# Moving a dispatch by four columns, splitting a weight conversion in three steps, and one stream for the expert weights

## The chip, the cores and the metric

The kernel runs on one core of one Trainium2 chip. The metric is the device time of one execution in microseconds (us); lower is better. The engines are PE (TensorE), DVE (VectorE), ACT (ScalarE), POOL (GpSimd) and SP (SyncE, which here only issues transfers).

## The reference

Three stages follow one another, all in float32. `q`, `k`, `v` are (8, 8, 576, 64); `T` is 4608 tokens, the model width is 512.

```
scores = scale * q_chunk @ k_chunk.T         # chunks of 64 tokens, each on its own
attn   = softmax(scores); x = attn @ v_chunk # -> x: (4608, 512)
h = x @ w_in                                 # (512, 2048)
g = h * sigmoid(1.702 * h)
y = g @ w_out                                # (2048, 512)
logits = y @ phi                             # 32 slots: 8 experts x 4
d = softmax(logits, axis=tokens)             # dispatch
slot_in  = d.T @ y                           # (32, 512)
slot_out = relu(slot_in[e] @ w1[e]) @ w2[e]  # each expert, 1024 wide
out = softmax(logits, axis=slots) @ slot_out # combine
```

## The kernel before, in words

**Blocks and columns.** The 4608 tokens are twelve blocks of 384 tokens. A block runs sixteen *columns* `f`, one for each 128 of the 2048 hidden units. `gemm(b, f)` (line 270) is 12 matmuls into one of three `h` banks (high part of the weight by high and low part of x, low part of the weight by high part of x), then a Tanh on ACT (L278) and one DVE instruction (L279) make the gated value. In the tables and in this text 2.4 is block 2, column 4.

**Order.** For the head and blocks 0 to 10 the order of instructions on each engine is the program's order. The tables `HEAD`, `SIDE0`, `SIDE1`, `SIDE2` (for the head and blocks 0 to 2) and `PLAN` (from block 2 on) say which extra step follows which column; `start` (L769) and `side` (L702) read them. In the last block and the tail only SP's order is given by hand. Each engine works strictly in order, so a step that waits holds all that stands behind it on its engine.

**Attention.** Three chunk pairs (`cp`) make a block. Scores (`attn_s`, L203) go to a pair tile `sx` of two banks, DVE takes the maximum and subtracts it (L211, L212), ACT takes Exp (L220), DVE sums, adds epsilon and inverts (L222 to L225), POOL or DVE multiplies (L226), PE transposes (L237), ACT copies, PE multiplies by v (`attn_x`, L251), ACT and DVE write the high and low part of x (L264, L265). In the head, `two_scores` (L763, step `R`) puts the scores of pairs 0 and 1 in one pair tile, so each bank holds both pairs.

**Conversion of w_in.** The weights come as 64-bit words. `w_in_a` (L141): ACT L118, then DVE L119 (shift) and L122 (shift and or). `w_in_b` (L144): ACT L147 copies the high part, POOL L148 subtracts it to make the low part. In block 0, column f is followed by `w_in_b(f+3)` and then `w_in_a(f+4)` (L798 to L802). The steps `i` and `j` in `HEAD` are the same two. `start_sel` (step `s`, L740) builds a small selection matrix on DVE; it is first used in 1.3.

**Dispatch.** g of a finished block is transposed on DVE (L289), stored to DRAM (L296, SP), read back in another layout (`load_g`, L304, four transfers of 768 KB on SP), and multiplied by the slot weights in `dispatch` (L468): 12 times two PE instructions, whose first ones read the transfer that was issued last. Block 0's `load_g` stands behind 2.0 and its dispatch, step `D`, behind 2.4. Block 1's stand behind 2.5 (`g0`) and 2.12 (`d0`); for later blocks it is the same two columns of the block that follows.

**Expert weights.** `load` (L517) fills a tile with the next units of `units` (the order in which the tail reads them); each run of neighbouring units in `w1` or `w2` is a transfer of its own, nearly all issued by POOL (L539, L545). w1 and w2 lie in DRAM as [128, expert, ...], each partition's row 128 KiB long. `TABLE` says where tiles are loaded; in the tail `used` (L551) refills a tile when its last unit is read. `combine` (L676) runs once for each half of the output: PE L688, copies on DVE and ACT, and six transfers of 768 KB, on POOL for the first half and on SP for the second.

Of the kernel before, what the change touches and what calls it, by code (L numbers as in the profile page):

```python
# [8 lines left out]
F32 = mybir.dt.float32  # L9
# [27 lines left out]
HEAD = "z q0 q1 q2 Li0 v0 v1 v2 Li1 R e0 i0 P2,- e1 i1 b0 j0 e2r P-,0 b1 j1 b2 P-,1 P-,2 Li2 q3 Li3 v3 Li4 q4 i2 j2 i3"  # L37
SIDE0 = {
    0: "P3,- Li5 v4 Li6", 1: "e3 q5", 2: "Li7 v5", 3: "P4,- b3 Li8", 4: "e4 phi Li9", 5: "Li10 q6", 6: "P5,3 Li11 v6",
    7: "e5 b4 Li12", 8: "Li13 q7", 9: "P6,4 Li14 v7", 10: "e6 b5 Li15", 11: "s Lo0r", 12: "P7,5 Lo1r", 13: "e7 b6 Lo2r", 14: "Lo3r",  # L40
# [7 lines left out]
SIDE2 = {0: "S2 g", 1: "S3", 3: "S4", 4: "D"}  # L48
# [4 lines left out]
def attention_moe_softmoe_kernel(  # L53
# [8 lines left out]
    w1: bass.AP,  # L62
    w2: bass.AP,
# [5 lines left out]
    E, F = w1.shape[1], w1.shape[2] * 128  # L69
# [7 lines left out]
    KE = F // 128  # L77
# [37 lines left out]
    def to_f32(a, st):  # L115
        f = st.bitcast(F32).rearrange("p (n w) -> p n w", w=2)
        u = st.bitcast(U32).rearrange("p (n w) -> p n w", w=2)
        nc.scalar.activation(out=a, in_=f[:, :, 1], func=ACTF.Prelu, scale=2.0 ** -112, alpha=-(2.0 ** 32))  # L118
# [768 lines left out]
```

## Time and profile before

| what | us |
|---|---|
| median of 3 runs (lowest to highest) | 682.08 (681.12 to 682.31) |
| the profiled execution | 681.62 |
| its span, first to last instruction | 679.8 |
| PE busy | 619.9 |
| DVE busy | 453.2 |

Times of instructions are counted from the start of the span. A bracket behind a row of a timeline is the idle time of that engine just before, and what ended it.

### The profile page before, as it was taken

How to read it: one execution, taken by the hardware profiler on the slowest of the kernel's cores; microseconds unless marked ns; L12 is line 12 of the kernel's file. 1: busy time of each engine (PE TensorE's matmuls, PEld its weight loads, DVE VectorE, ACT ScalarE, POOL GpSimd, SP SyncE). 2: the span in 40 equal slices, each digit the busy share in tenths (PEclk: the TensorE clock that was granted, in tenths of full speed). 3: DMA queues.
4: the chain of work that ended last, by engine and by line, in shares of the span. 5: the costliest groups of instructions: out<-in, count | busy, mean ns of one | idle time of the engine just before them, and what ended most of it. 6: DMA issues, size and time to landing. Idle time of an engine off the chain costs nothing.

```text
span 679.8 us, 15616 instructions
## 1 busy us (share of the span) xinstructions
PE 619.9 (91%) x6414; PEld 522.1 (77%) x6414; DVE 453.2 (67%) x972; ACT 225.6 (33%) x469; POOL 115.2 (17%) x160
## 2 busy tenths in 40 slices
PE   3797899994999999999999999999999999978891
PEld 3685766792989899898998998989989898736550
DVE  5688789791867778778677786776876736331132
ACT  3446444330324234233333332323423322111141
POOL 2253300000100000000000010000010222454640
PEclk9999999996999999999999999999999999999996
DMA  9934867669656749478486585774938879889998
GB/s 348 352 94 140 279 189 247 182 152 350 234 170 225 247 147 347 120 230 285 136 290 210 160 322 157 237 234 151 346 97 230 292 233 396 295 276 369 369 402 341
DMA packets 67798, 167.94 MB, mean 247 GB/s; under 512 B 13200, under 2 KB 36880, under 8 KB 67728
## 3 DMA queue, kind: packets, MB, share of 16 engines
q1 hardware_dynamic: 57376, 129.72, 57.8%
q0 software_dynamic: 10352, 37.23, 15.0%
q8 instruction: 50, 0.82, 0.5%
q14 instruction: 20, 0.16, 0.1%
HBM read 122.29 MB, written 44.63 MB: 246 GB/s over the span
## 4 chain that ended last, share of the span: by engine, by line
PE 77%; DVE 10%; DMA 5%; ACT 3%; issue 2%; POOL 0%; SPq 0%; DVEq 0%; ACTq 0%; POOLq 0%
PE h L274 18%; PE h L276 17%; PE h L275 17%; PE dtg L474 5%; PE lp L340 5%; PE sx L203 3%; DVE cv L122 2%; PE sx L251 2%; PE h1p L635 2%; PE pt L237 2%; DVE cv L119 2%; DMA g<-g_dram 1%; DVE gt L279 1%; DMA out_dram<-o 1%; PE fp L655 1%
## 5 line engine op out<-in xcount | busy, mean ns | idle before, releaser
L274 PE MATMUL h<-xh,w 128*128 128x384 f32 x768 | 266.0, 346 | 3.1 <-ACT w L147 2.4
L276 PE MATMUL h<-xh,w 128*128 128x384 f32 x768 | 258.8, 337 | 7.4 <-POOL w L148 7.4
L275 PE MATMUL h<-xl,w 128*128 128x384 f32 x768 | 258.0, 336 | 0.0
L278 ACT ACTIVATE gt<-h 128x384 f32<-128x384 f32 x192 | 94.1, 490 | 234.5 <-PE h L276 234.3
L274 PEld LDWEIGHTS h<-xh,w 128*128 128x128 f32 x768 | 144.7, 188 | 22.6 <-issue 17.5
L279 DVE SCALAR_TENSOR_TENSOR gt<-gt,h 128x384 f32<-128x384 f32 x192 | 104.9, 547 | 82.8 <-ACT gt L278 82.4
L276 PEld LDWEIGHTS h<-xh,w 128*128 128x128 f32 x768 | 144.7, 188 | 10.2 <-POOL w L148 9.3
L275 PEld LDWEIGHTS h<-xl,w 128*128 128x128 f32 x768 | 144.9, 189 | 0.4 <-DVE xl L265 0.4
L226 POOL TENSOR_TENSOR e<-e,rs 128x512 f32<-128x512 f32 x35 | 36.6, 1047 | 443.5 <-DVE rs L225 440.9
L289 DVE STREAM_TRANSPOSE g<-gt 128x384 f32<-128x384 f32 x176 | 100.1, 574 | 5.4
L264 ACT ACTIVATE xh<-sx 128x512 fp32r<-128x512 f32 x36 | 21.5, 599 | 95.8 <-DVE e L212 82.2
L474 PE MATMUL dtg<-g,dt 128*32 128x512 f32 x288 | 35.1, 622 | 10.5 <-DMA g<-g_dram 9.1
L265 DVE TENSOR_TENSOR xl<-sx,xh 128x512 fp32r<-128x512 f32 x36 | 24.8, 690 | 26.6 <-ACT xh L264 24.5
L340 PE MATMUL lp<-gt,wp 128*32 128x384 f32 x384 | 36.8, 492 | 0.1
L474 PEld LDWEIGHTS dtg<-g,dt 128*32 128x32 f32 x288 | 9.5, 114 | 30.8 <-issue 29.2
L539 POOL DMA_DIRECT2D w<-in_moe_w_dram x44 | 23.6, 542 | 53.4 <-PE h L276 23.6
L545 POOL DMA_DIRECT2D w<-in_moe_w_dram x53 | 28.4, 538 | 17.6 <-DMA w<-in_moe_w_dram 10.3
L211 DVE TENSOR_REDUCE mx<-sx 128x8 f32<-128x512 f32 x36 | 23.7, 659 | 7.0 <-PE sx L203 7.0
L122 DVE SCALAR_TENSOR_TENSOR cv<-stg,cv 128x512 uint32<-128x512 uint32 x32 | 27.2, 851 | 1.1
L148 POOL TENSOR_TENSOR w<-cv,w 128x512 fp32r<-128x512 f32 x16 | 22.9, 1443 | 23.7 <-ACT w L147 23.7
L237 PE MATMUL pt<-ident,e 128*128 128x128 f32 x144 | 23.1, 286 | 3.7 <-POOL e L226 2.1
L212 DVE TENSOR_TENSOR e<-sx,mx 128x512 f32<-128x512 f32 x36 | 24.9, 691 | 1.8
(118 smaller groups left out, 560.5 us busy)
## 6 DMA issues: line engine op xcount, KB each, us to landing
g_dram<-g SPq DMA_DIRECT2D x176, 192.0 KB, 3.7
g<-g_dram SPq DMA_DIRECT2D x44, 768.0 KB, 8.3
w<-in_moe_w_dram POOLq DMA_DIRECT2D x70, 256.0 KB, 5.5
qk<-in_qk_dram SPq DMA_DIRECT2D x30, 512.0 KB, 5.6
w<-in_moe_w_dram POOLq DMA_DIRECT2D x27, 512.0 KB, 7.3
stg<-in_moe_w_in_dram SPq DMA_DIRECT2D x16, 512.0 KB, 8.2
stg<-in_moe_w_out_t_dram SPq DMA_DIRECT2D x16, 512.0 KB, 5.5
wo<-in_moe_w_out_dram SPq DMA_DIRECT2D x16, 512.0 KB, 3.7
```

What stands on the lines that cost most here:

```text
L122: nc.vector.scalar_tensor_tensor(out=a.bitcast(U32), in0=u[:, :, 0], scalar=29, in1=a.bitcast(U32), op0=ALU.logical_shift_right, op1=ALU.b ...
L226: (nc.gpsimd if pool else nc.vector).tensor_tensor(out=e, in0=e, in1=rs.to_broadcast([128, 2 * KD, 64]), op=ALU.mult)
L237: nc.tensor.transpose(p[:, hp, :], e[:, 2 * hp:2 * hp + 2, :].rearrange("p h k -> p (h k)"), ident)
L274: nc.tensor.matmul(out=h, lhsT=a, rhs=xh[b][:, k, :], start=(k == 0), stop=False)
L275: nc.tensor.matmul(out=h, lhsT=a, rhs=xl[b][:, k, :], start=False, stop=False)
L276: nc.tensor.matmul(out=h, lhsT=l, rhs=xh[b][:, k, :], start=False, stop=(k == KD - 1))
L278: nc.scalar.activation(out=t, in_=h, func=ACTF.Tanh, scale=0.851)
L279: nc.vector.scalar_tensor_tensor(out=t, in0=t, scalar=1.0, in1=h, op0=ALU.add, op1=ALU.mult)
L289: nc.vector.transpose(out=g1[b, q][:, :, :, 32 * j:32 * (j + 1)], in_=t.rearrange("p (a b c) -> p b a c", b=4, c=32))
L340: nc.tensor.matmul(out=lp[b][32 * j:32 * (j + 1), :], lhsT=wp[:, f, :], rhs=gt[b, f], start=(g == 0), stop=(g == NG - 1),)
L474: nc.tensor.matmul(out=p[32 * j:32 * (j + 1)], lhsT=dt[:, i, :], rhs=g[j][i], start=(i == 0), stop=(i == NCP - 1))
L545: eng.dma_start(out=v, in_=w2[:, key[1], key[2], c:c + m])
```

## The change

- `D` moves from behind 2.4 to behind 2.8; in block 2 alone `g0` moves from column 5 to 9 and `d0` from 12 to 15.
- The conversion of w_in is three steps: `w_in_a` (ACT L118), `w_in_b` (the two DVE instructions), `w_in_c` (ACT copy, POOL subtraction). Behind column f of block 0 stand a(f+5), b(f+4), c(f+3), in that order; the transfers of the weights stand up to one column earlier.
- In the head `R` is replaced by `A0 A1r A2` (scores) and `C0r C1 C2r` (products with v). Those with `r` use two `h` banks, and their evictions go in two halves, one for each bank; the others use the pair tile. The multiplications of pairs 0 and 1 (`e0r`, `e1r`) go from POOL to DVE. The conversion of the second weight tile stands behind `C2r`.
- `start_sel` moves from 0.11 to 1.1, with one broadcast copy in place of four.
- w1 and w2 become one array w12 of [128, 65536] in the order of use; `load` issues one transfer for a tile. Each partition's row is now 256 KiB long.

The core of the diff (left out: the arguments of the kernel, `attn_x`, which indexes its two banks the same way as `attn_s`, and the lines of `start` that call `first`):

```diff
@@ -34,18 +34,18 @@
...
-HEAD = "z q0 q1 q2 Li0 v0 v1 v2 Li1 R e0 i0 P2,- e1 i1 b0 j0 e2r P-,0 b1 j1 b2 P-,1 P-,2 Li2 q3 Li3 v3 Li4 q4 i2 j2 i3"
+HEAD = "z q0 q1 q2 Li0 v0 v1 v2 Li1 A0 A1r i0 e0r A2 e1r I0 b0 e2r j0 C0r i1 b1 C1 b2 C2r I1 j1 Li2 q3 Li3 v3 Li4 q4 i2 i3 I2 j2 i4 I3"
 SIDE0 = {
-    0: "P3,- Li5 v4 Li6", 1: "e3 q5", 2: "Li7 v5", 3: "P4,- b3 Li8", 4: "e4 phi Li9", 5: "Li10 q6", 6: "P5,3 Li11 v6",
-    7: "e5 b4 Li12", 8: "Li13 q7", 9: "P6,4 Li14 v7", 10: "e6 b5 Li15", 11: "s Lo0r", 12: "P7,5 Lo1r", 13: "e7 b6 Lo2r", 14: "Lo3r",
+    0: "P3,- Li5 v4 Li6 Li7", 1: "e3 q5", 2: "Li8 v5", 3: "P4,- b3 Li9", 4: "e4 phi Li10", 5: "Li11 q6", 6: "P5,3 Li12 v6",
+    7: "e5 b4 Li13", 8: "Li14 q7", 9: "P6,4 Li15 v7", 10: "e6 b5", 11: "Lo0r", 12: "P7,5 Lo1r", 13: "e7 b6 Lo2r", 14: "Lo3r",
     15: "Lo4r",
...
 SIDE1 = {
-    0: "o0 o1 Lo5r Lo6r", 1: "o2 o3 Lo7r Lo8r", 2: "b7 c0 o4 o5 Lo9r Lo10r", 3: "d0 o6 o7 Lo11r Lo12r", 4: "P8,6 k0 l0 c1 o8 Lo13r",
+    0: "o0 o1 Lo5r Lo6r", 1: "s o2 o3 Lo7r Lo8r", 2: "b7 c0 o4 o5 Lo9r Lo10r", 3: "d0 o6 o7 Lo11r Lo12r", 4: "P8,6 k0 l0 c1 o8 Lo13r",
     5: "e8 d1 o9 o10 Lo14r Lo15r", 6: "o11 o12", 7: "c2 o13 o14 t0 t1", 8: "P9,7 k1 l1 d2 o15", 9: "e9 c3 t2 t3 t4", 10: "b8 d3 t5 t6 t7",
...
 }
-SIDE2 = {0: "S2 g", 1: "S3", 3: "S4", 4: "D"}
+SIDE2 = {0: "S2 g", 1: "S3", 3: "S4", 8: "D"}
 EPS = 1e-9
@@ -113,9 +111,15 @@
...
+        to_f32_a(a, st)
+        to_f32_b(a, st)
...
+    def to_f32_a(a, st):
...
+        nc.scalar.activation(out=a, in_=f[:, :, 1], func=ACTF.Prelu, scale=2.0 ** -112, alpha=-(2.0 ** 32))
...
+    def to_f32_b(a, st):
...
-        nc.scalar.activation(out=a, in_=f[:, :, 1], func=ACTF.Prelu, scale=2.0 ** -112, alpha=-(2.0 ** 32))
@@ -139,9 +143,13 @@
...
     def w_in_a(f):
-        iv[f] = conv("i", f)
+        iv[f] = pro[0].tile([128, DM], F32, tag="cv", name="cv", bufs=NCV)
+        to_f32_a(iv[f], stg["i", f])
...
     def w_in_b(f):
+        to_f32_b(iv[f], stg.pop(("i", f)))
+
+    def w_in_c(f):
         v = iv.pop(f).rearrange("p (k c) -> p k c", k=KD)
@@ -192,27 +200,34 @@
...
+    def each(p):
+        return [(slice(h, h + 1), p[h].rearrange("p (o x) -> p o x", o=1)) for h in range(2)] if isinstance(p, list) else [(slice(0, 2), p)]
...
-        p = p.rearrange("p h (a k) -> p h a k", k=64)
+        y = [p[h] if isinstance(p, list) else p[:, h, :] for h in range(2)]
+        y = [v.rearrange("p (a k) -> p a k", k=64) for v in y]
...
-                        out=p[w, h, hp, :], lhsT=t[r, 0, hp, w], rhs=t[r, 1, hp, w], start=True, stop=True
+                        out=y[h][w, hp, :], lhsT=t[r, 0, hp, w], rhs=t[r, 1, hp, w], start=True, stop=True
...
-        nc.vector.tensor_reduce(out=mx, in_=p, axis=AX.X, op=ALU.max)
-        nc.vector.tensor_tensor(
-            out=e.rearrange("p (a h) k -> p h a k", h=2), in0=p, in1=mx.to_broadcast([128, 2, KD, 64]),
-            op=ALU.subtract,
-        )
+        ev = e.rearrange("p (a h) k -> p h a k", h=2)
+        for hs, v in each(p):
+            v = v.rearrange("p h (a k) -> p h a k", k=64)
+            nc.vector.tensor_reduce(out=mx[:, hs], in_=v, axis=AX.X, op=ALU.max)
+            nc.vector.tensor_tensor(
+                out=ev[:, hs], in0=v, in1=mx[:, hs].to_broadcast(list(v.shape)), op=ALU.subtract
+            )
@@ -261,8 +277,10 @@
...
-        nc.scalar.activation(out=yh, in_=x, func=ACTF.Copy)
-        nc.vector.tensor_tensor(out=yl, in0=x, in1=yh.bitcast(F32), op=ALU.subtract)
+        for hs, v in each(x):
+            v = v.rearrange("p h (a c) -> p h a c", c=128)
+            nc.scalar.activation(out=yh[:, hs], in_=v, func=ACTF.Copy)
+            nc.vector.tensor_tensor(out=yl[:, hs], in0=v, in1=yh[:, hs].bitcast(F32), op=ALU.subtract)
@@ -533,19 +551,19 @@
...
         for key, c, m in runs:
+            live |= {key + (c + z,) for z in range(m)}
             if key[0] == 1:
...
                 at += m * DM
-                eng.dma_start(out=v, in_=w1[:, key[1], c:c + m])
                 for z in range(m):
...
                 at += m * DH
-                eng.dma_start(out=v, in_=w2[:, key[1], key[2], c:c + m])
                 for z in range(m):
                     w2_t[key[1], key[2], c + z] = v[:, z, :]
-            live |= {key + (c + z,) for z in range(m)}
+        eng.dma_start(out=t[:, 0:at], in_=w12[:, w_at[0]:w_at[0] + at])
+        w_at[0] += at
         slots.append((kind, live))
@@ -701,6 +719,8 @@
...
+            if b == 2:
+                at = {"g0": 9, "d0": 15}.get(name, at)
@@ -742,8 +762,7 @@
...
-        for j in range(4):
-            nc.vector.tensor_copy(sel[:, j, :], t)
+        nc.vector.tensor_copy(sel, t.rearrange("p (o s) -> p o s", o=1).to_broadcast([128, 4, 32]))
@@ -760,20 +779,24 @@
...
-    def two_scores():
-        t = pair_tile("sx")
-        y = [attn_s(cp, t[:, :, 256 * cp:256 * cp + 256]) for cp in range(2)]
-        for cp in range(2):
-            attn_m(cp, y[cp])
+
+    def first(step, cp, alt):
+        p = [ps_h.tile([128, 256], F32, tag="h", name="sx") for _ in range(2)] if alt else pair_tile("sx")[:, :, 0:256]
+        if step == "A":
+            attn_s(cp, p)
+            attn_m(cp, p)
+        else:
+            attn_x(cp, p)
+            attn_y(cp, p)
...
         fns = {
-            "i": w_in_a, "j": w_in_b, "o": wp_a, "q": load_qk, "v": load_v, "b": attn_b, "c": wp_c, "d": wp_d,
+            "i": w_in_a, "I": w_in_b, "j": w_in_c, "o": wp_a, "q": load_qk, "v": load_v, "b": attn_b, "c": wp_c, "d": wp_d,
             "t": lambda f: store_g(0, f), "k": lambda g: logits(0, g), "l": lambda g: logits(1, g),
...
         once = {
-            "R": two_scores, "phi": start_wp, "z": start_const, "s": start_sel, "g": lambda: load_g(0), "D": lambda: dispatch(0),
+            "phi": start_wp, "z": start_const, "s": start_sel, "g": lambda: load_g(0), "D": lambda: dispatch(0),
         }
@@ -796,10 +821,9 @@
...
             if b == 0:
-                if f + 3 < NF:
-                    w_in_b(f + 3)
-                if f + 4 < NF:
-                    w_in_a(f + 4)
+                for step, n in ((w_in_a, f + 5), (w_in_b, f + 4), (w_in_c, f + 3)):
+                    if n < NF:
+                        step(n)
             if b == NB - 1 and f:
@@ -848,6 +872,8 @@
...
+    w1 = w1.reshape(e // 4, 4, d // 128, 128, nf // 256, 2, 128).transpose(3, 0, 4, 1, 5, 2, 6).reshape(128, -1)
+    w2 = w2.reshape(e // 4, 4, nf // 512, 4, 128, 2, d // 2).transpose(4, 5, 0, 2, 1, 3, 6).reshape(128, -1)
@@ -855,8 +881,7 @@
...
-        "in_moe2_w1_dram": w1.reshape(e, d // 128, 128, nf // 128, 128).transpose(2, 0, 3, 1, 4),
-        "in_moe2_w2_dram": w2.reshape(e, nf // 128, 128, 2, d // 2).transpose(2, 3, 0, 1, 4),
+        "in_moe2_w12_dram": np.concatenate([w1, w2], axis=1),
```

## Rows read from the trace of the kernel before

**Rows 1.** The page, parts 1 and 2: busy time; clock in 40 slices

```profile
PE 619.9 (91%) x6414; PEld 522.1 (77%) x6414; DVE 453.2 (67%) x972; ACT 225.6 (33%) x469; POOL 115.2 (17%) x160
...
PEclk9999999996999999999999999999999999999996
```

**Rows 2.** Waits of PE: line, for whom, us in total, times, longest

```profile
PE dtg L474 <- DMA g<-g_dram: 9.1, 1, 9.1
PE h L276 <- POOL w L148: 7.4, 6, 1.7
...
PE wpp L160 <- DVE cv L122: 1.5, 2, 1.1
```

**Rows 3.** Timeline of PE, 2.4 to 2.9: start, us, line [idle before]

```profile
162.44 4.68 PE L474 MATMUL dtg<-g,dt 128*32 128x512 f32 x24 [9.11 <-DMA g<-g_dram]
167.05 0.44 PE L274 MATMUL h<-xh,w 128*128 128x384 f32 x1
...
177.01 0.45 PE L274 MATMUL h<-xh,w 128*128 128x384 f32 x1
```

**Rows 4.** Windows: PE PEld DVE ACT POOL busy, granted clock, DMA share, GB/s

```profile
150.00:155.00 5.00, 3.33 (x85) 1.93 (x83) 4.08 (x11) 1.32 (x3) 0.00 (x0) 1.00 0.99 269
...
160.00:165.00 5.00, 2.56 (x13) 0.71 (x17) 0.00 (x0) 0.00 (x0) 0.00 (x0) 0.50 0.93 321
```

**Rows 5.** Chain that ended last: the dispatch of the last block

```profile
601.08 2.90 PE dtg L474 x24
```

**Rows 6.** Timeline of the SP queue around the start of block 2

```profile
150.19 2.92 SPq L308 DMA_DIRECT2D g<-g_dram  x4
```

**Rows 7.** Timeline of DVE in the head

```profile
15.18 1.41 DVE L122 SCALAR_TENSOR_TENSOR cv<-stg,cv 128x512 uint32<-128x512 uint32 x1
...
18.09 0.69 DVE L226 TENSOR_TENSOR e<-e,rs 128x512 f32<-128x512 f32 x1
```

**Rows 8.** Timeline of PE at the end of the head

```profile
22.45 1.13 PE L251 MATMUL sx<-pt_sb,qv 64*64 64x64 f32 x32 [1.44 <-DVE xl L265]
24.30 0.69 PE L274 MATMUL h<-xh,w 128*128 128x384 f32 x1 [0.72 <-ACT xh L264]
```

**Rows 9.** Timeline of DVE in block 0, 53 to 66 us

```profile
53.00 1.06 DVE L119 TENSOR_SCALAR cv<-cv 128x512 uint32<-128x512 uint32 x1 [0.38 <-ACT cv L118]
54.10 0.69 DVE L122 SCALAR_TENSOR_TENSOR cv<-stg,cv 128x512 uint32<-128x512 uint32 x1
...
56.21 0.38 DVE L119 TENSOR_SCALAR cv<-cv 128x512 uint32<-128x512 uint32 x1
56.62 1.41 DVE L122 SCALAR_TENSOR_TENSOR cv<-stg,cv 128x512 uint32<-128x512 uint32 x1
...
59.34 1.37 DVE L119 TENSOR_SCALAR cv<-cv 128x512 uint32<-128x512 uint32 x1 [0.85 <-ACT cv L118]
...
65.02 1.06 DVE L119 TENSOR_SCALAR cv<-cv 128x512 uint32<-128x512 uint32 x1 [0.38 <-ACT cv L118]
```

**Rows 10.** Waits of DVE, 24 to 80 us

```profile
DVE cv L119 <- ACT cv L118: 4.5, 6, 1.3
```

**Rows 11.** Timeline of DVE, column 11 of block 0

```profile
70.84 1.76 DVE L746 CAST sel<-acc 128x32 fp32r<-128x32 f32 x4
```

**Rows 12.** Timeline of PE, last combine

```profile
659.78 5.59 PE L688 MATMUL op<-sr,ct 32*128 32x256 f32 x72 [0.47 <-ACT sr L665]
```

**Rows 13.** Timeline of the SP queue in the tail

```profile
662.32 6.84 SPq L700 DMA_DIRECT2D out_dram<-o  x6
```

**Rows 14.** Windows of the tail, columns as in rows 4

```profile
630.00:640.00 10.00, 9.00 (x156) 5.16 (x148) 0.85 (x2) 1.15 (x3) 6.70 (x14) 1.00 1.03 386
...
664.00:674.00 10.00, 1.38 (x16) 0.65 (x10) 2.48 (x6) 1.82 (x5) 0.00 (x0) 0.70 1.02 424
```

**Rows 15.** DMA queues, 605 to 651 us, then 664 to 665: packets, MB, share

```profile
q0 software_dynamic: 4644, 15.83, 94.6%
...
q1 hardware_dynamic: 7, 0.04, 10.2%
```

More of the change, by code (lines that the diff above doesn't have):

```diff
@@ L61, in attention_moe_softmoe_kernel @@
     phi: bass.AP,
-    w1: bass.AP,
-    w2: bass.AP,
+    w12: bass.AP,
     out: bass.AP,
@@ L68, in attention_moe_softmoe_kernel @@
     DFF = w_out.shape[1] * 128
-    E, F = w1.shape[1], w1.shape[2] * 128
     NS = phi.shape[1]
@@ L76, in attention_moe_softmoe_kernel @@
     NG = NF // GF
-    KE = F // 128
+    KE = w12.shape[1] // (NS // 4 * 2 * DM)
     DH = DM // 2
@@ L243, in attn_x @@
         t, p = v_t.pop(cp), pt.pop(cp)
-        x = x.rearrange("p h (a c) -> p h a c", c=128)
+        y = [x[h] if isinstance(x, list) else x[:, h, :] for h in range(2)]
+        y = [v.rearrange("p (a c) -> p a c", c=128) for v in y]
         for c in range(2):
@@ L251, in attn_x @@
                         nc.tensor.matmul(
-                            out=x[64 * z:64 * z + 64, h, a, w], lhsT=t[r, 2 * a + z, w], rhs=p[r, 2 * a + z, w],
+                            out=y[h][64 * z:64 * z + 64, a, w], lhsT=t[r, 2 * a + z, w], rhs=p[r, 2 * a + z, w],
                             start=True, stop=True,
@@ L514, in attention_moe_softmoe_kernel @@
     ]
-    slots = []
+    slots, w_at = [], [0]
     def load(kind, eng):
@@ L783, in start @@
                 load_w(x[1], int(n[1:]), x[-1] == "r")
+            elif k in "AC":
+                first(k, int(n), x[-1] == "r")
             elif k == "P":
```

## The prediction, made before the changed kernel was run

> **What bounds the kernel now.** I read the busy shares first. PE is busy 91% of the span [rows 1], so time can come only from its gaps, from a slow clock, or from the two ends where PE is not the bound. The line of granted clocks says where to look: nines, except one slice near 170 us and the last one [rows 1]. The list of PE's waits then names the gaps: one wait of 9.1 us of the dispatch for g, six waits of 7.4 us in all for POOL's low part of w_in, and 1.5 us for converted w_out in block 1 [rows 2]. From block 2's dispatch to the tail the list holds nothing else, so what is gained ahead of 2.9 reaches the end undiminished. The tail is another matter: there the DMA engines are full while PE waits for no weight.
>
> **Sum.** The sum is made against the profiled execution, 681.62 us (span 679.8, and 1.8 around it). The median of the runs shown is 0.46 above it.
>
> **Part 1, the dispatch, -10.8.** In 2.4 PE stands for 9.11 us until block 0's g has landed, at 162.44 [rows 3]. The granted clock in 160 to 165 is 0.50, its lower level, 1.2 GHz, after that pause [rows 4]; the dispatch takes 162.44 to 167.05, 4.61 us [rows 3], where the last block's, at full clock, takes 2.90 [rows 5]. Pause and slow clock cost 9.11 + 1.71 = 10.82. With `D` behind 2.8, PE fills the time with columns 5 to 8: 167.05 to 177.01 is 9.96 us of work, a pair step among it [rows 3]. PE left off at 162.44 - 9.11 = 153.33 and comes to the dispatch at 163.29, 0.85 after the landing. The transfers are issued at the same point of the program as before (from 150.19, behind 2.0 [rows 6]), and what is ahead of them on SP is the same, so the whole 10.82 goes. The cover is thin: each us by which g lands later than 163.3 costs one, and more if the clock falls; the bound is a landing 3 us late, so -7.8 to -10.8. Moved along with it: `g0` needs the four tiles that `D` frees, so SP waits for the dispatch and then issues behind 2.9; behind it on SP are block 2's stores of column 11 and the ct stores. `d0` follows six columns later, at least 6/4 of 9.96, about 15 us, while the first load took 162.44 - 150.19 = 12.25 in a crowded stretch. That edit and the bank of the accumulator (free again by column 10) cost nothing; without that cover the wait would return in 2.15 as a few us.
>
> **Part 2, the head, -1.5.** DVE runs without a break from the first scores to the last multiplication at 18.09 [rows 7]. Out of that chain goes the second weight's conversion, 0.38 [rows 9] + 1.41 [rows 7] = 1.8; and as POOL no longer multiplies beside it, the first conversion's `or` takes 0.69 [rows 9] in place of 1.41, 0.7 less. Into it come two multiplications of 0.69 [rows 7], 1.4, and second halves of evictions, about 0.2. Net -0.9. At the end PE waits 1.44 for the low part of pair 1 before pair 2's product, because both use the same banks [rows 8]; with `C2r` in other banks that wait goes. Against both: ACT now has weight 0's first step ahead of the first Exp and weight 1's ahead of the copy of pair 1's transposed scores; a step of this size on 512 columns is not shorter than 0.69 on DVE [rows 9], so I charge 0.8. -0.9 - 1.4 + 0.8 = -1.5. Bounds: nothing, if ACT becomes the chain, to -2.6. The first gemm starts near 22.8 in place of 24.30 [rows 8].
>
> **Part 3, block 0, -2.4.** Every three columns (one pair) the pattern repeats: the same DVE shift starts at 53.00 and at 65.02, 12.02 us [rows 9]. In it DVE waits for ACT's first step 0.38 and 0.85 [rows 9], since that step is queued behind the Tanh of the same column. Issued one column earlier, it is done by then: 1.2 a period. The other loss of the period stays: where POOL works at the same time, the shift takes 1.06 or 1.37 in place of 0.38, and the `or` 1.41 in place of 0.69 [rows 9]; the same instructions still meet. PE's waits for POOL are what this chain leaves behind [rows 2], and they start in column 6, when the lead of converted weights is used up; so of the 4.5 us of such waits [rows 10] only those of two periods count: -2.4. Next late is `w_in_c`: in a pair's column ACT's copy stands behind the eviction of x, which waits for DVE. Bounds: 0 (port and eviction order set the pace) and -4.5 (all these waits). The move of `s` frees 2 us of DVE in column 11 [rows 11], where PE waits for POOL's product rather than for DVE's end; nothing.
>
> **Part 4, block 1, +0.6.** `s` now runs in 1.1, ahead of the conversion of w_out for 1.2, for which PE waits up to 1.1 [rows 2]. One copy of 128 elements and one reduction: four copies took 1.76, one of them stretched by POOL [rows 11]; two short DVE instructions are about 0.6. Bounds 0 and +1.1.
>
> **Part 5, the expert stream, -0.8.** From 605 to 651 POOL's queue moves 15.83 MB [rows 15], with the engines full, at 386 GB/s in the window 630 to 640, while the output, in rows of 6 KB and with fewer transfers, runs at 424 [rows 14]. About 100 transfers of 256 and 512 KB become some 60 of 512 and 768 KB. At 424 the 46 us would shrink by up to 46 x (1 - 386/424) = 4.1. But the last copies follow PE's combine at 659.78 [rows 12], which waits for no weight, and SP issues the last outputs from 662.32 [rows 13]. Their first packets show in 664 to 665 [rows 15], about 2.4 later; if nothing stood before them they could flow perhaps 1.2 earlier, and then the 4.7 MB take their 11 us at 424 as before. So of 4.1 at most 1.2 is seen; I take 0.8. Bounds +1.5 (the planner of the last block orders PE by other transfers) and -1.5.
>
> One rule speaks against this part. In the rows a stream with a partition pitch of 128 KiB runs at 386 [rows 14]; 256 KiB is not in the trace. The Trainium skill, "DMA: Bandwidth & Descriptors", section "Latency and other measured facts", says that row pitches of large powers of two slow copies: 512 KiB gave 207 GB/s where 214 is full. By that, as an estimate, the stream would take at most 3% longer, 1.4 us of 46, and the sum would be about 1.4 to 2 higher.
>
> Together: -10.8 - 1.5 - 2.4 + 0.6 - 0.8 = -14.9. 681.62 - 14.9 = 666.7, and 0.46 more for the median: **667.2**.
>
> **Rivals.**
> *The port takes it back.* Head and block 0 gain nothing: 667.2 + 3.9 = 671.1. For it: the stretched shifts and `or`s, which the split does not remove. Against: the waits for ACT are separate rows. 0.20.
> *PE-paced block 0.* All 7.4 us of waits for POOL go, not 2.4: 662.2. For it: PE is free in them. Against: 1.2 a period is all that leaves the DVE chain. 0.13.
> *Half of the dispatch's wait stays*, because g lands late beside the stores of 2.7: +5.5, 672.7. For it: 0.85 us of margin, and engines at a share of 0.93 to 0.99 [rows 4]. 0.08.
> *The dispatch moves and does nothing:* g is held until PE is there, all 10.8 stay: 678.0. Against: SP issued at 150.19 without PE [rows 6]. 0.02.
> *Slower: the stream from w12 is slow.* Place: POOL's queue from 605 on. The same full engines once moved 269 GB/s [rows 4]; at that rate 15.83 MB take 58.8 us, +12.8 on 46, and the sum is 667.2 + 0.8 + 12.8 = 680.8. It decides below 15.83 / (46 + 15) = 260; at 250 the time is 685. For it: every partition's row starts at a multiple of 256 KiB. Against: the stream ran at 386 with half that pitch. 0.04. The rule of the Trainium skill named under part 5 points this way, but not this far.
>
> **How the numbers follow.** The forecast, with its parts inside their bounds, has 0.5, and its own range is 663 to 671; the rest, 0.03, are mishaps of no one place. A measurement of this kernel can tell 0.2%, 1.4 us, from no change. Range: from 661.5, which takes in the PE-paced block, to 673.5, which takes in the port and half the wait; outside are the slow stream, the idle dispatch, the mishaps and the far ends, under 2 in 10. Faster 0.93: all but the slow stream and part of the mishaps; same 0.02; slower 0.05.
>
> **What would show it.** Part 1: no wait of PE for g in block 2, no fall of the clock there, 10 us between block 2's column 4 and 9 without a gap. Part 2: the first gemm near 22.8. Part 3: a period of 10.8 in place of 12.0, no DVE wait for ACT's first step, waits for POOL's product still there. Part 4: DVE idle elsewhere, the first w_out product waiting up to 1.7. Part 5: 400 GB/s or more in the stream, the last SP outputs at the same distance from the last combine. A wait for g in 2.8 or 2.15, a stream under 350, or PE waiting for weights would make it wrong.

## The result and the profile after

The changed kernel takes 664.73 us (median of 3 runs, 664.66 to 665.85) where the one before takes 682.08: a ratio of 0.9754, 95% interval 0.9732 to 0.9776. The forecast was 667.2, the range 661.5 to 673.5. The profiled execution of after took 665.85 (span 664.1), that of before 681.62 (span 679.8): 15.77 less.

Where it came from is read best by stages. The table gives, from the profiled execution of each kernel that ran, the start of the first gemm, the start of ACT's Tanh in some columns, the distance from the last Tanh (11.15) to the second combine (`op`), and from there to the end of the span, all in us. The experiments, which are described further down, stand in it already; their ratio is to the kernel before on the same chip, where it had medians of 680.16 (e1 to e4), 680.35 (c to e8) and 680.85 (e9 to e12).

| kernel | median | ratio | first gemm | 0.6 | 0.9 | 0.15 | 1.4 | 3.0 | 11.15 to op | op to end |
|---|---|---|---|---|---|---|---|---|---|---|
| before | 682.08 | 1 | 24.30 | 47.13 | 59.21 | 80.12 | 95.56 | 200.16 | 63.83 | 20.02 |
| after | 664.73 | .9754 | 22.34 | 45.53 | 56.18 | 75.89 | 91.90 | 185.84 | 65.42 | 17.01 |
| e1 dispatch back | 674.98 | .9921 | 22.24 | 45.44 | 56.09 | 75.81 | 91.80 | 196.09 | 64.05 | 16.84 |
| e2 two steps | 669.34 | .9841 | 22.43 | 47.56 | 59.58 | 80.30 | 96.30 | 190.73 | 65.33 | 17.05 |
| e3 old head | 666.34 | .9790 | 24.28 | 46.21 | 56.86 | 76.57 | 92.56 | 186.52 | 65.24 | 17.03 |
| e4 two arrays | 668.12 | .9823 | 22.53 | 45.73 | 56.36 | 76.08 | 92.09 | 186.01 | 65.30 | 19.38 |
| c, after again | 664.74 | .9764 | 22.40 | 45.60 | 56.25 | 75.97 | 91.97 | 185.90 | 63.97 | 17.08 |
| e5 split transfers | 667.62 | .9806 | 22.42 | 45.61 | 56.28 | 75.99 | 91.97 | 185.91 | 63.84 | 20.69 |
| e7 row pitch | 664.74 | .9762 | 22.33 | 45.50 | 56.55 | 75.83 | 91.82 | 185.97 | 63.84 | 17.43 |
| e8 dispatch at 7 | 668.54 | .9822 | 22.33 | 45.52 | 56.17 | 75.89 | 91.88 | 188.91 | 65.31 | 16.58 |
| e9 s in 0.15 | 664.68 | .9764 | 22.41 | 45.62 | 56.64 | 75.99 | 91.44 | 185.39 | 63.85 | 17.28 |
| e10 low on DVE | 664.06 | .9763 | 22.21 | 45.63 | 56.55 | 75.55 | 91.55 | 185.54 | 63.89 | 17.03 |
| e11 copy first | 662.77 | .9744 | 22.47 | 45.68 | 56.33 | 74.29 | 89.74 | 183.69 | 63.85 | 17.64 |
| e12 copy first, low 1 in 3 | 661.07 | .9709 | 22.28 | 44.79 | 55.43 | 72.82 | 88.28 | 182.21 | 63.85 | 17.46 |

After against before: -4.23 at 0.15, -3.66 at 1.4, -14.32 at 3.0, and the same to 0.04 at 11.15; then +1.59 to the second combine and -3.01 from there to the end. The sum is -15.7, the difference of the spans.

Each row is one execution, and a single column of block 0 can come 0.4 later in one than in another: e7 and e9, which run block 0 up to 0.14 as after does, have 0.9 at 56.55 and 56.64 (the granted clock was 0.57 in 54 to 58 there, 1.00 in after), and 0.15 within 0.1 of after. A period is read more safely from DVE's rows.

The page of after, busy time and the clock in 40 slices, answers [rows 1]:

```profile
PE 620.1 (93%) x6414; PEld 523.4 (79%) x6414; DVE 455.0 (69%) x975; ACT 225.3 (34%) x471; POOL 92.2 (14%) x117
...
PEclk9999999999999999999999999999999999998997
```

PE does the same work in 16 us less; the dip in the slice of 153 to 170 us is gone, and a small one has come near 600. Its waits, for [rows 2]:

```profile
PE h L294 <- POOL w L156: 5.5, 5, 1.6
...
PE h L292 <- ACT w L155: 2.2, 3, 1.0
...
PE wpp L168 <- DVE cv L126: 1.7, 3, 1.1
```

There is no wait for g any more; those for the low part of w_in fell from 7.4 to 5.5 only. The timeline of PE at the end of the head, for [rows 8] (first row), and behind column 8 of block 2, for [rows 3]:

```profile
22.34 0.69 PE L292 MATMUL h<-xh,w 128*128 128x384 f32 x1 [0.49 <-ACT xh L282]
...
158.49 0.69 PE L216 MATMUL sx<-qk 64*64 64x64 f32 x32
159.01 0.65 PE L267 MATMUL sx<-pt_sb,v 64*64 64x64 f32 x32
159.59 2.78 PE L492 MATMUL dtg<-g,dt 128*32 128x512 f32 x24
162.30 0.44 PE L292 MATMUL h<-xh,w 128*128 128x384 f32 x1
```

The dispatch starts right behind the pair step and takes 2.78, as the last block's does at full clock. One period of block 0 on DVE, for [rows 9]:

```profile
51.22 0.42 DVE L123 TENSOR_SCALAR cv<-cv 128x512 uint32<-128x512 uint32 x1
...
53.79 0.37 DVE L123 TENSOR_SCALAR cv<-cv 128x512 uint32<-128x512 uint32 x1
54.20 1.41 DVE L126 SCALAR_TENSOR_TENSOR cv<-stg,cv 128x512 uint32<-128x512 uint32 x1
...
56.00 1.05 DVE L123 TENSOR_SCALAR cv<-cv 128x512 uint32<-128x512 uint32 x1
57.09 1.67 DVE L126 SCALAR_TENSOR_TENSOR cv<-stg,cv 128x512 uint32<-128x512 uint32 x1
...
61.28 0.69 DVE L283 TENSOR_TENSOR xl<-sx,xh 128x512 fp32r<-128x512 f32 x1 [0.72 <-ACT xh L282]
61.89 0.42 DVE L123 TENSOR_SCALAR cv<-cv 128x512 uint32<-128x512 uint32 x1
```

From 51.22 to 61.89 is 10.67 where it was 12.02. No shift in it waits for ACT's first step now (of the 4.5 us of [rows 10] one wait of 1.3 is left, ahead of this stretch); the stretched ones are still there. The windows of the tail (columns as in [rows 4]), for [rows 14], and the second combine and the last outputs' issue, for [rows 12, 13]:

```profile
598.00:600.00 2.00, 2.00 (x34) 1.93 (x30) 0.33 (x5) 0.00 (x0) 0.00 (x0) 0.50 1.02 405
600.00:602.00 2.00, 1.98 (x33) 1.65 (x26) 0.00 (x0) 0.38 (x1) 0.30 (x1) 0.65 1.03 367
...
630.00:640.00 10.00, 9.39 (x134) 6.13 (x138) 5.54 (x10) 5.26 (x12) 3.53 (x7) 1.00 1.03 411
```

```profile
647.09 5.60 PE L706 MATMUL op<-sr,ct 32*128 32x256 f32 x72 [0.47 <-ACT sr L683]
...
649.62 6.00 SPq L718 DMA_DIRECT2D out_dram<-o  x6
```

The stream runs at 411 GB/s in place of 386. But the window 630 to 640 is 20 to 30 us ahead of the second combine in before and 7 to 17 in after; at after's distance before ran at 372:

```profile
642.69:652.69 10.00, 9.39 (x134) 6.12 (x138) 5.53 (x10) 5.26 (x12) 7.13 (x14) 1.00 1.00 372
```

The 1.6 us that the tail lost is the granted clock: 0.50 and 0.65 in 598 to 602, while the first products with the expert weights ran.

### The profile page after: what moved, and what is told of

It is laid out like the page before. It is cut to its first block, busy times and chain, and to the rows that moved or that the text cites. A ratio compares the mean times of both kernels' runs of the same rounds, so it can differ in the third digit from the quotient of the medians.

```text
span 664.1 us, 15558 instructions
## 1 busy us (share of the span) xinstructions
PE 620.1 (93%) x6414; PEld 523.4 (79%) x6414; DVE 455.0 (69%) x975; ACT 225.3 (34%) x471; POOL 92.2 (14%) x117
## 3 DMA queue, kind: packets, MB, share of 16 engines
q0 software_dynamic: 8608, 37.23, 14.8%
## 4 chain that ended last, share of the span: by engine, by line
PE 81%; DVE 9%; ACT 3%; issue 2%; DMA 2%; SPq 0%; POOL 0%; DVEq 0%; ACTq 0%
PE h L292 19%; PE h L294 18%; PE h L293 18%; PE lp L358 5%; PE dtg L492 5%; PE sx L216 3%; PE h1p L653 3%; DVE cv L126 2%; PE sx L267 2%; PE fp L673 2%; PE pt L252 2%; DVE cv L123 2%; DVE gt L297 1%; PE op L706 1%; DMA v<-in_v_dram 1%
## 5 line engine op out<-in xcount | busy, mean ns | idle before, releaser
L241 POOL TENSOR_TENSOR e<-e,rs 128x512 f32<-128x512 f32 x33 | 34.5, 1044 | 415.9 <-DVE rs L240 410.5
L282 ACT ACTIVATE xh<-sx 128x512 fp32r<-128x512 f32 (+1 forms) x38 | 21.6, 575 | 96.0 <-DVE e L228 82.4
L283 DVE TENSOR_TENSOR xl<-sx,xh 128x512 fp32r<-128x512 f32 (+1 forms) x38 | 25.0, 661 | 25.3 <-ACT xh L282 23.8
L565 POOL DMA_DIRECT2D w<-in_moe_w_dram x56 | 29.8, 533 | 87.0 <-PE h L294 36.2
L492 PE MATMUL dtg<-g,dt 128*32 128x512 f32 x288 | 33.2, 594 | 1.4 <-DVE dt L450 1.4
L126 DVE SCALAR_TENSOR_TENSOR cv<-stg,cv 128x512 uint32<-128x512 uint32 x32 | 29.7, 928 | 1.1
L227 DVE TENSOR_REDUCE mx<-sx 128x8 f32<-128x512 f32 (+1 forms) x37 | 23.9, 645 | 5.7 <-PE sx L216 5.7
L228 DVE TENSOR_TENSOR e<-sx,mx 128x512 f32<-128x512 f32 (+1 forms) x37 | 25.1, 677 | 1.8
L715 DVE COPY o<-op 128x512 f32<-128x512 f32 (+1 forms) x20 | 11.1, 630 | 21.1 <-PE op L706 21.1
```

Of the source, the lines that this page charges most:

```text
L126: nc.vector.scalar_tensor_tensor(out=a.bitcast(U32), in0=u[:, :, 0], scalar=29, in1=a.bitcast(U32), op0=ALU.logical_shift_right, op1=ALU.b ...
L241: (nc.gpsimd if pool else nc.vector).tensor_tensor(out=e, in0=e, in1=rs.to_broadcast([128, 2 * KD, 64]), op=ALU.mult)
L492: nc.tensor.matmul(out=p[32 * j:32 * (j + 1)], lhsT=dt[:, i, :], rhs=g[j][i], start=(i == 0), stop=(i == NCP - 1))
L565: eng.dma_start(out=t[:, 0:at], in_=w12[:, w_at[0]:w_at[0] + at])
```

## The experiments

**e1, the dispatch where it was.**

```diff
-SIDE2 = {0: "S2 g", 1: "S3", 3: "S4", 8: "D"}
+SIDE2 = {0: "S2 g", 1: "S3", 3: "S4", 4: "D"}
...
-            if b == 2:
-                at = {"g0": 9, "d0": 15}.get(name, at)
```

> The changed kernel with the dispatches and the load of g back in their old columns (behind 2.4, 2.5 and 2.12); the rest of the change stays. Theory (the parts add up): the wait of 9 us for g and the half clock return, nothing else moves; 664.7 + 10.7 = 675.4 us. Rival (the earlier start of block 2 also brought the landing of g nearer, so part of the wait had gone anyhow): a wait of 4 to 6 us, about 670.

Measured: 674.98, ratio 0.9921 (0.9903 to 0.9939). At 3.0 it is 10.25 behind after, and the wait and the slow slice are back:

```profile
PE dtg L492 <- DMA g<-g_dram: 8.8, 1, 8.8
```

```profile
PEclk9989999996999999999999999999999999999997
```

So the parts add: the dispatch is worth 10.3 to 10.7 of the 17, and the rival, a wait of 4 to 6, falls.

**e2, the conversion in two steps again, with the new head.**

```diff
-                for step, n in ((w_in_a, f + 5), (w_in_b, f + 4), (w_in_c, f + 3)):
+                for step, n in ((w_in_c, f + 3), (w_in_a, f + 4), (w_in_b, f + 4)):
```

(and the end of `HEAD` as "i2 I2 j2 i3 I3")

> The changed kernel with the conversion of w_in in two steps again (behind column f: high and low part of f+3, then ACT's and DVE's steps of f+4 together). Theory: DVE waits again 1.2 us for ACT's first step in each period of three columns, periods of 12.0 in place of 10.7, and two of them count: +2.5, 667.2 us. Rival (block 0 gained by start_sel leaving column 11 and by the earlier weight transfers): no more than +0.5, 665.2.

Measured: 669.34, ratio 0.9841 (0.9821 to 0.9862). The period is 12.0 again (47.56 to 59.58; DVE's shift 53.36 to 65.37), and column 0.15 comes at 80.30, no earlier than before the change: +4.4 on after, more than the +2.5 expected. `s` is out of column 11 in e2 too, so the rival, by which that move and the earlier transfers made the gain, falls. PE's wait for POOL's part:

```profile
PE h L294 <- POOL w L156: 7.9, 7, 1.7
```

The head's lead of 1.87 at the first gemm is spent by column 6, and the new head without the three steps is worth nothing.

**e3, the old head, with the three steps.**

```diff
-HEAD = "z q0 q1 q2 Li0 v0 v1 v2 Li1 A0 A1r i0 e0r A2 e1r I0 b0 e2r j0 C0r i1 b1 C1 b2 C2r I1 j1 ...
+HEAD = "z q0 q1 q2 Li0 v0 v1 v2 Li1 R e0 i0 I0 P2,- e1 i1 I1 b0 j0 e2r P-,0 b1 j1 b2 P-,1 P-,2 ...
```

(left out: `two_scores`, put back)

> The changed kernel with the first three pairs as before (scores of pairs 0 and 1 in one pair tile, multiplications of 0 and 1 on POOL, second weight converted in the chain). Theory: the first gemm starts 2.0 later, and column 6 of block 0 as well by 1.6, so 666.3 us. Rival (PE waits for converted weights later anyhow, so the head's gain is lost in block 0): the first gemm 2.0 later, but the last column of block 0 within 0.4 of the changed kernel, 664.9.

Measured: 666.34, ratio 0.9790 (0.9767 to 0.9812). The first gemm starts at 24.28, 1.94 later than in after, but only 0.68 of it is left in 0.6 and stays so to 3.0: not the 1.6 of the theory, more than the 0.4 of the rival. The three steps alone give 3.55 at 0.15 (80.12 to 76.57), the head on top of them 0.68.

**e4, two weight arrays, a transfer for each run of experts,** as before the change.

```diff
+                eng.dma_start(out=v, in_=w1[:, key[1], c:c + m])
...
+                eng.dma_start(out=v, in_=w2[:, key[1], key[2], c:c + m])
...
-        eng.dma_start(out=t[:, 0:at], in_=w12[:, w_at[0]:w_at[0] + at])
-        w_at[0] += at
```

(left out: the arguments, and the layout of the two arrays in DRAM, as before)

> The changed kernel with w1 and w2 as two arrays and one transfer for each run of units, as before. From the start of the last combine to the end of the span it was 20.0 us before and 17.0 in the changed kernel. Theory: that distance goes back to 20.0, the rest stays, +3.0: 667.7 us against 664.7. Rival (the prediction's term): +0.8, 665.5, the distance below 18.

Measured: 668.12, ratio 0.9823 (0.9805 to 0.9842). Up to 3.0 it is after (186.01); from the second combine to the end it takes 19.38 in place of 17.01, near the theory's 20.0 and not below the 18 of the prediction's term.

**c, the changed kernel again; e5, one array, but a transfer for each run.**

```diff
+                eng.dma_start(out=t[:, at:at + m * DM], in_=w12[:, w_at[0] + at:w_at[0] + at + m * DM])
                 at += m * DM
...
+                eng.dma_start(out=t[:, at:at + m * DH], in_=w12[:, w_at[0] + at:w_at[0] + at + m * DH])
                 at += m * DH
...
-        eng.dma_start(out=t[:, 0:at], in_=w12[:, w_at[0]:w_at[0] + at])
```

> The changed kernel itself, unchanged, so that the others stand against it on this chip. 0.975 of the kernel before. Whether the granted clock falls behind the second dispatch of the last block (0.50 for some 2 us in the profiled execution of the result) differs between executions by the first theory: with the fall about 1.2 us more from the last Tanh to the combine, without it the distance is 64 as before. The rival, that the new order itself makes the fall, expects it in every execution.

> The weights lie as in the changed kernel, but each run of experts is again a transfer of its own (about a hundred of 256 and 512 KB). First theory, the number and size of the transfers set the stream's rate: it falls to about 385 GB/s, the last output queue stands behind weights again, and from the second combine to the end it takes 19.4 us as with two arrays (17.0 in the changed kernel); the time is 2.4 us above the changed kernel. Rival, the single array with the weights in the order of use is what makes it faster: 17.0 and no change.

Measured: c 664.74, ratio 0.9764 (0.9746 to 0.9783); e5 667.62, ratio 0.9806 (0.9788 to 0.9823). The window of the stream and q0's packets, MB and share over the whole span, first of c:

```profile
630.00:640.00 10.00, 9.44 (x137) 6.08 (x138) 5.54 (x10) 5.17 (x11) 3.45 (x7) 1.00 1.03 413
```

```profile
q0 software_dynamic: 8608, 37.23, 14.8%
```

and of e5:

```profile
630.00:640.00 10.00, 9.44 (x138) 5.96 (x138) 5.54 (x10) 5.17 (x11) 6.60 (x13) 1.00 1.01 365
```

```profile
q0 software_dynamic: 10352, 37.23, 15.3%
```

With the engines full in both (shares 1.01 and 1.03), e5 moves 365 GB/s, c 413: packets of 3.6 KB on average (37.23 MB in 10352) against 4.3 KB. The rate falls further than to the 385 expected, and the time at the end, 20.69, is above the 19.4. The same holds for a longer stretch, the 46 us that [rows 15] show for before (there 15.83 MB), at the same distance from the second combine: q0 in 591 to 637, first of c, then of e5:

```profile
q0 software_dynamic: 3957, 17.02, 95.9%
...
q0 software_dynamic: 4654, 15.85, 94.7%
```

So the number and size of the transfers make the rate, and the single array alone gains nothing: e4 and e5, with 19.38 and 20.69 from the second combine to the end, lie on either side of the 20.02 before the change. Which of number and size it is, was not told apart. Why that shows at the end is seen in the queues of three single microseconds. In after, with the outputs issued at 649.62, q0 in 649 to 650 and q1 (the outputs) in 650 to 651:

```profile
q0 software_dynamic: 13, 0.04, 10.6%
...
q1 hardware_dynamic: 39, 0.24, 57.7%
```

In e5, issued at 648.15, the same two queues in 650 to 651:

```profile
q0 software_dynamic: 68, 0.39, 92.8%
q1 hardware_dynamic: 3, 0.02, 4.4%
```

The outputs of e5 were issued 1.5 us earlier and flow later, because q0 still holds the engines. In c, with the outputs issued at 648.26, q1 had a share of 0.91 already in 649 to 650.

What q0 holds then is not weights: it is the first half's outputs, which POOL issues behind its last weights. Their issue, first in before, then in c, then in e5:

```profile
651.11 0.54 POOL L700 DMA_DIRECT2D out_dram<-o  x1 [0.19 <-issue]
652.81 2.90 POOL L700 DMA_DIRECT2D out_dram<-o  x5 [1.16 <-DMA w<-in_moe_w_dram]
...
633.25 1.11 POOL L718 DMA_DIRECT2D out_dram<-o  x2 [3.02 <-ACT o L713]
...
637.50 0.54 POOL L719 DMA_DIRECT2D out_dram<-o  x1 [0.18 <-issue]
639.27 2.84 POOL L719 DMA_DIRECT2D out_dram<-o  x5 [1.22 <-DMA w<-in_moe_w_dram]
```

They start 8.7 us ahead of the second combine in before, 12.5 in c and 8.1 in e5, and the last of the six lands at 668.9, 649.8 and 655.2; the second half's first output, issued at 662.32, 648.26 and 648.15, lands 7.0, 3.4 and 7.3 later. With merged transfers POOL is done with the weights before the first half's copies are, without them five of the six outputs wait, by these rows, for a landing of weights.

The clock of the first products of the last block, in c:

```profile
598.00:600.00 2.00, 2.00 (x58) 2.00 (x58) 0.42 (x6) 0.02 (x1) 0.00 (x0) 1.00 1.05 399
600.00:602.00 2.00, 1.89 (x44) 1.42 (x40) 0.42 (x1) 0.36 (x1) 1.43 (x3) 1.00 1.01 357
```

Full, with the same instructions in the same order, and the distance to the second combine is 63.97, as before the change. The rival falls: the new order does not make the dip in every execution. Whether it makes it more frequent is not shown; of before there is one trace.

**e7, rows 260 KiB apart.**

```diff
-    KE = w12.shape[1] // (NS // 4 * 2 * DM)
+    KE = 8
...
-        "in_moe2_w12_dram": np.concatenate([w1, w2], axis=1),
+        "in_moe2_w12_dram": np.concatenate([w1, w2, np.zeros((128, 1024), np.float32)], axis=1),
```

> The rows of the weight array stand 260 KiB apart in place of 256 KiB, and nothing else is changed. By the rule of the Trainium skill on row pitches of large powers of two (page DMA: Bandwidth & Descriptors) the stream would run up to 3% faster, 418 to 423 GB/s in place of 406 to 411, and the last outputs would land up to 1 us earlier. My theory: no difference within 0.7 us and within 5 GB/s.

Measured: 664.74, ratio 0.9762 (0.9742 to 0.9782), the same time as c to 0.01. The stream:

```profile
630.00:640.00 10.00, 9.44 (x138) 5.93 (x134) 5.54 (x10) 5.17 (x11) 3.76 (x7) 1.00 1.03 412
```

412 with the padded rows, 413 without in the same window of c. The row of the Trainium skill ("DMA: Bandwidth & Descriptors", section "Latency and other measured facts"), read down to 256 KiB, would have had the padded rows faster; a pitch of 256 KiB shows no such loss here. Its own figure is for 512 KiB, which was not run.

**e8, the dispatch one column earlier.**

```diff
-SIDE2 = {0: "S2 g", 1: "S3", 3: "S4", 8: "D"}
+SIDE2 = {0: "S2 g", 1: "S3", 3: "S4", 7: "D"}
```

> Block 1's second dispatch stands one column earlier, behind column 7 of block 2. It measures how late g may land. The prediction had PE at the dispatch 0.85 us after the landing; a column with its pair step is some 3.2 us, one without 2.1. If the margin is 0.85, PE waits 1.2 to 2.4 us for g and the time is as much longer. If g lands earlier than that now (the chip has more time between stores), PE waits less than 0.5 and nothing is lost. If the stores of block 2 beside it delay it, the wait is above 3.

Measured: 668.54, ratio 0.9822 (0.9803 to 0.9841); column 3.0 comes 3.0 us later than in c. The dispatch on PE, and the issue of g on SP:

```profile
159.28 2.78 PE L492 MATMUL dtg<-g,dt 128*32 128x512 f32 x24 [2.85 <-DMA g<-g_dram]
```

```profile
146.30 3.29 SPq L326 DMA_DIRECT2D g<-g_dram  x4
```

PE stands for 2.85, above the 1.2 to 2.4 of the theory, and starts on g at 159.28, 12.98 after its first issue. How late g may land in after has to be read in after itself, since SP issues 0.29 earlier there and the transfers take 0.2 less. SP's issue, and the fourth transfer alone, issued at 148.59:

```profile
146.01 3.07 SPq L326 DMA_DIRECT2D g<-g_dram  x4
...
DMA to landing us min/median/max: 10.1/10.1/10.1
```

It lands at 148.59 + 10.1 = 158.7, and PE, which in before and e8 starts 0.13 to 0.14 after the landing, comes at 159.59: a margin of about 0.8. It is thin: in e7 PE comes 0.16 after the landing, and in e2 it waits 0.2. So column 8 costs next to nothing and column 7 costs 3.0. The clock stays at full speed through e8's shorter pause (1.00 in 155 to 160 and in 160 to 165).

**e9, `s` in 0.15.** (Before the change it stood in 0.11; the expectation's "where it stood before" is wrong.)

```diff
-    15: "Lo4r",
+    15: "s Lo4r",
-    ... 1: "s o2 o3 Lo7r Lo8r",
+    ... 1: "o2 o3 Lo7r Lo8r",
```

> The selection step s goes back from column 1 of block 1 to column 15 of block 0, where it stood before, and the rest stays as changed. Part 4 of the prediction, tested alone: block 1 gives back its 0.57 us (from the distance -4.23 at 1.2 to -3.66 from 1.3 on), and column 0.15 is not later by more than 0.2: -0.6 at 3.0, the time about 0.999 of the changed kernel. Rival: DVE is the bound of block 0 to its end and the two microseconds of s come back there: no gain, or +0.5.

Measured: 664.68, ratio 0.9764 (0.9745 to 0.9783), against c's 0.9764: half a microsecond is below what the runs can tell. The trace tells it: 75.99 at 0.15, no later than c, and 91.44 at 1.4 against 91.97. Part 4's cost is 0.53 there, and 0.51 are left of it at 3.0, where 0.6 was expected.

**e10, every low part on DVE.**

```diff
-        nc.gpsimd.tensor_tensor(out=t[:, 1], in0=v, in1=t[:, 0].bitcast(F32), op=ALU.subtract)
+        nc.vector.tensor_tensor(out=t[:, 1], in0=v, in1=t[:, 0].bitcast(F32), op=ALU.subtract)
```

> The low part of every w_in weight is formed by DVE in place of POOL, and nothing else is changed. Theory, the stretched shifts and ors of block 0 (1.05 in place of 0.38, 1.41 and 1.68 in place of 0.69) are what POOL's work at the same time costs DVE: per period some 2.4 us of stretch go and three subtractions of 0.69 come, 2.1, so the period goes from 10.67 to about 10.3 and column 0.15 comes 0 to 1.5 us earlier; no or takes over 1.0 except beside the pair's multiplication. Rival, the stretch has another cause (the operands, the ACT engine): it stays, and the period grows by 2.1 to about 12.7, column 0.15 comes 6 to 8 us later.

Measured: 664.06, ratio 0.9763 (0.9739 to 0.9788). DVE, in the same stretch of block 0 as shown for after:

```profile
50.92 0.42 DVE L123 TENSOR_SCALAR cv<-cv 128x512 uint32<-128x512 uint32 x1
...
54.15 0.38 DVE L123 TENSOR_SCALAR cv<-cv 128x512 uint32<-128x512 uint32 x1
54.56 1.42 DVE L126 SCALAR_TENSOR_TENSOR cv<-stg,cv 128x512 uint32<-128x512 uint32 x1
55.90 0.68 DVE L156 TENSOR_TENSOR w<-cv,w 128x512 fp32r<-128x512 f32 x1
...
56.97 0.42 DVE L123 TENSOR_SCALAR cv<-cv 128x512 uint32<-128x512 uint32 x1
57.42 0.69 DVE L126 SCALAR_TENSOR_TENSOR cv<-stg,cv 128x512 uint32<-128x512 uint32 x1
58.03 0.69 DVE L156 TENSOR_TENSOR w<-cv,w 128x512 fp32r<-128x512 f32 x1
...
61.84 0.42 DVE L123 TENSOR_SCALAR cv<-cv 128x512 uint32<-128x512 uint32 x1
```

The shift at 56.97 takes 0.42 and the `or` 0.69 (1.05 and 1.67 in after); only the `or` beside the pair's multiplication, which POOL still does, takes 1.42. So the stretch is POOL's doing. The Trainium skill says the same ("SBUF — State Buffer", section "SBUF: two separate sides"): DVE and GpSimd share a pair of ports; when a DVE instruction that uses the pair and a GpSimd instruction meet, the one that starts first holds it to its end, and the other waits; these rows agree, with 0.42 against 1.05 and 0.69 against 1.67. The period is 10.92 (the shift at 50.92 to that at 61.84): not the 12.7 of the rival, nor the 10.3 of the theory, which had counted the `or` beside the multiplication as freed too. Column 0.15 comes 0.42 earlier than in c, inside what the theory gave. POOL's three low parts cost DVE 1.6 a period (0.63 + 0.98), and done on DVE they take 2.06; the period grew by 0.25, so having them on POOL saves DVE little.

**e11, in pair columns the copy ahead of the pair step; e12, and one low part in three on DVE.**

```diff
+            early = b == 0 and f and f % 3 == 0 and f + 3 < NF
+            if early:
+                w_in_c(f + 3)
             if b < 3:
                 start((SIDE0, SIDE1, SIDE2)[b].get(f, ""))
...
-                    if n < NF:
+                    if n < NF and not (early and step is w_in_c):
```

(both with `s` as in e9), and in e12

```diff
-        nc.gpsimd.tensor_tensor(out=t[:, 1], in0=v, in1=t[:, 0].bitcast(F32), op=ALU.subtract)
+        (nc.vector if f % 3 == 1 else nc.gpsimd).tensor_tensor(out=t[:, 1], in0=v, in1=t[:, 0].bitcast(F32), op=ALU.subtract)
```

> In the columns 3, 6, 9 and 12 of block 0 the copy and low part of the weight of three columns on stand ahead of the pair step in program order, not behind it, and s is back in 0.15. The prediction named this copy as the next one late: it stands behind the eviction of x on ACT, which waits for DVE. Theory: PE's waits for POOL's low part and ACT's copy of w_in (7.7 us in all) shrink, 0.3 to 0.5 us a period at 0.12 while DVE stays the bound; with s some -1.0 us in all, 0.9985 of the changed kernel. Rival: DVE's chain sets the period alone and earlier copies change nothing in block 0: only the 0.6 of s.

> As the one before, and of the low parts one in three (the weights 1, 4, 7, ...) is formed by DVE, 0.69 us, in place of POOL. If POOL's pairs of low parts right behind one another (3.2 us in the trace) hold up both the ors on DVE and PE, the period falls by a further 0.2 to 0.5 and the whole is -1.2 to -2 us against the changed kernel. Rival: DVE is the bound and each subtraction adds its 0.69 to the period: column 0.15 comes 1 to 2 us later than with the copies first alone.

Measured: e11 662.77, ratio 0.9744 (0.9719 to 0.9768); e12 661.07, ratio 0.9709 (0.9693 to 0.9726). The period does not move in either: 10.66 and 10.62 by DVE's shift (51.37 to 62.03 and 50.40 to 61.02). Earlier copies leave it alone, as e11's rival says, and in e12 the subtraction on DVE takes no more than the stretch it saves. What they gain lies at the two ends of block 0. Level with c at 0.9, e11 is 1.7 ahead at 0.15, and PE's waits for ACT's copy (0.9 us in c, 2.2 in after) are gone; of the waits that after still has behind column 12, 0.32 for ACT's copy at 72.48 and 0.76 for POOL at 73.85, e11 has none. So the rest of the rival, that block 0 gains nothing, falls. e12 is 0.8 ahead of c from column 6 on and 3.15 at 0.15, and PE's waits for the low part, 4.5 us of POOL's in c, have become

```profile
PE h L294 <- DVE w L156: 4.0, 3, 2.0
```

e12 is 3.69 ahead of c at 3.0 and 3.67 in the time; the two intervals of the ratio don't touch. That is more than the 1.2 to 2 that its theory gave, and its rival, 0.15 later than in e11, falls: it comes 1.47 earlier. It beats both kernels. What e11 alone is worth its runs don't settle: its interval overlaps c's, though its trace is 2.2 ahead at 3.0, where its theory had 1.0.

## Why the prediction was right, and where its terms were not

**Part 1, right.** -10.8 was forecast; from 2.4 to 3.0 the distance grows by 10.66, and e1 takes 10.25 back. The slow clock went with the pause. The margin was forecast at 0.85 and is about 0.8, but by two differences that cancel: from the first issue of g to its use there are 13.58 us (159.59 - 146.01) where the prediction had 13.10 (163.29 - 150.19), and g lands 0.5 later after that issue than in before. So the rival by which half of the wait stays fell, by little, and the one by which the dispatch does nothing fell by far.

**Parts 2 and 3, right in their sum and wrong in the split.** -1.5 and -2.4 make -3.9; measured -4.23 at 0.15. The first gemm moved by 1.96 rather than 1.5. But "the first gemm near 22.8" is no gain at the end of block 0, since the next columns wait for weights that DVE converts at its own pace: e2 has all of that lead and arrives no earlier than before, e3 has none of it and loses only 0.68. So the head's -1.5 is -0.68 at 0.15, and the three steps' -2.4 is -3.55 (e3). Their period was forecast at 10.8 and is 10.67; the step that failed in part 3 is "only those of two periods count: -2.4". Two periods, 0.6 to 0.12, do give 2.7 (24.10 to 21.38), and the rest, 0.92 in e3, comes ahead of column 6, where the prediction saw a lead that wasn't used up. "The other loss of the period stays" was right, and e10 shows that POOL causes it. So the rival of a block 0 paced by PE fell (5.5 us of waits for POOL are left), and so did that of a port that takes it back.

**Part 4, right.** +0.6 forecast, +0.57 between 0.15 and 1.4, and e9 gets 0.53 of it back.

**Part 5, right in its direction, far too small.** -0.8 forecast, bounds to -1.5; from the second combine to the end -3.01. The rate rose as thought, to 411. The step that failed is "if nothing stood before them they could flow perhaps 1.2 earlier, and then the 4.7 MB take their 11 us". It took half of the 2.4 us between issue and first packets [rows 13, 15] for a fixed delay; with a nearly empty q0 the outputs flow within 1.4 of their issue, at a share of 0.58. In before they were far behind that: q1's share was 0.10 in 664 to 665, 0.70 in 665 to 666 and 0.90 in 666 to 667, with q0 still at 0.89, 0.37 and 0.09. What stood before them were the first half's outputs, which the prediction did not name, and their first landing came 3.7 us sooner after its issue (3.3 for 7.0). e4 and e5 put the term back by undoing the merge, e5 by that alone. The rates in the sum don't go together either: 386 GB/s is all queues in an early window, the 15.83 MB in 46 us are 344 on q0 alone, and the 4.1 and the slow rival's 12.8 mix the two.

**What no part had.** +1.59 from the last Tanh to the second combine, the dip of the clock. It is in the profiled execution of after and not in that of c, which is the same kernel; the two other runs of after were 1.1 to 1.2 shorter. Against the median the parts therefore come to -17.35, 2.5 below the forecast, nearly all of it part 5's. That the two profiled executions differ by 15.77, so near to the 14.9 of the sum, is in part luck: the dip, +1.59, hides most of the 2.2 that part 5 missed.

**The slower rival** (a slow stream from w12) fell: the stream ran faster than the old one, and e7 shows no price of the pitch.

## What to carry over

Count a lead at the start of a stage only if the engine that paces the stage gets it too: here DVE's period decided, and PE's earlier start was spent within six columns. Where outputs are issued behind a stream and the last outputs share the DMA engines with them, a faster stream pays even if no engine waits for its data; the queues in the microseconds around the last issue show it. Work on POOL beside DVE isn't free when DVE is the bound: measure what it adds to DVE's own instructions before calling it offloaded.

## What the hardware showed that was not expected

- With the DMA engines full in both (share 1.01 to 1.03), q0's 37.23 MB, in packets of 3.6 KB (e5) and 4.3 KB (c), went with 365 and 413 GB/s over all queues in the same window, 630 to 640.
- The granted clock fell to 0.50, 1.2 GHz, for about 3 us behind the last block's dispatch in the profiled executions of after, e2, e3, e4 and e8, and not there in those of before, c and the others. The distance from 11.15 to the second combine is 65.2 to 65.4 with it and 63.8 to 64.1 without. PE was busy 0.77, 2.00, 1.52 and 1.25 us in the four windows of 2 us from 590 in after, and 0.69, 2.00, 1.61 and 1.16 in c; what decides it stays open. In block 0 too one execution has a slow stretch where another of the same kernel has none (c 0.68 in 45 to 50 and 0.77 in 65 to 70, after 1.00 in both), and there it costs nothing: 0.15 comes at 75.97 and 75.89.
- A pause of PE of 8.8 to 9.1 us in block 2 was followed by half the clock (before, e1), one of 2.85 at nearly the same place was not (e8).
